# Attention and a cosine feed-forward on one core: plain float32 products for nine pairs of heads, and scalings moved between engines

## The chip, the cores and the metric

The kernel runs on one core of a Trainium2 chip. The metric is the device time of one execution in microseconds (us). Five engines work side by side, each through its own queue in order: PE (matrix products; PEld are its weight loads), DVE (vector), ACT (scalar, with the exponent), POOL (GpSimd), and SP, which here only issues transfers. Products are written to PSUM, the other tiles lie in SBUF.

## The reference

Eight batches, twelve heads, 448 positions, head size 64. q and k are divided by the root mean square of their rows and multiplied by g_q and g_k, then comes attention, then a feed-forward layer whose activation is h cos(h):

```python
rms = np.sqrt(np.mean(x * x, axis=-1, keepdims=True) + 1e-06)   # q_n, k_n = x / rms * g
scores = scale * np.matmul(q_n, k_n.transpose(0, 1, 3, 2))
attn = np.exp(scores - np.max(scores, axis=-1, keepdims=True))
attn = attn / (np.sum(attn, axis=-1, keepdims=True) + 1e-09)
x = np.matmul(attn, v)              # to [3584, 768]
h = x @ w_in                        # [3584, 2048]
y = (h * np.cos(h)) @ w_out         # [3584, 768]
```

## The kernel before

The 96 heads are worked on as 48 pairs, two heads side by side in the 128 partitions; six pairs make one batch b. The program has two parts. The first holds attention of all pairs and the first feed-forward product (L571 to L573) of batches 0 to 6, whose blocks lie between the attention pieces of the next batch; the second (from about 940 us) holds the product of the last batch, the activation and the second product (L646 to L648).

**Precision.** A matrix product with float32 accuracy is made in one of two ways. Split: both operands are cut into a part rounded to float32r (hi) and the remainder (lo), and three products hi·hi, lo·hi, hi·lo are summed. Plain: one product of float32 tiles, with no remainders to prepare. `S32` lists the pairs whose scores are plain, `A32` those whose product P v is plain. Before, these are pairs 0 and 1, and 0 to 11.

**Preparation of a pair** (`prepare(u)`, from pair 2; pairs 0 and 1 take a path of their own, `first(u)`). ACT squares the rows of q and k, DVE sums them (L298), POOL adds the mean's 1e-6 (L302) and takes the power -1/2 (L306). SP stores these factors and loads them back spread over all partitions (`rkb` for k, `rqb` for q). Then POOL multiplies k by its factors (L370), ACT casts k to hi (L373), POOL makes its remainder `kl` (L377). For q POOL first multiplies by g_q g_k / 8 with a minus sign (`q_scale`, L385, in place), then by its factors (L389); ACT casts it to `qhi` (L392), POOL makes `ql` (L396). A pair in `S32` has no `kl`, `ql` and no casts: POOL writes `khi` and `qhi` itself. `kd`, `qd`, `rkb`, `rqb` have one buffer each, `khi`, `qhi`, `kl`, `ql` two.

**Attention of a pair** (`attend(u)`). Seven tiles of scores: column group j holds the tiles j and j + 4, tile 3 stands alone (L438); three PSUM banks and one shared with the feed-forward hold them. DVE takes the minimum of each row (L447; the scores carry a minus sign), ACT the exponent with the row sum (L456). `rsum` adds 1e-9 to the row sums (L463) and inverts them (L464), both on DVE. Then four blocks kc of 128 keys: PE transposes P into `PT` (L481), which has one buffer of two halves; for a plain pair ACT copies the first half to SBUF (L492) and DVE the second (L490), and PE multiplies by v (L520). For a split pair ACT casts both halves, DVE makes the remainders `lo` (L500, L502), and PE multiplies both (L512); v is cut by POOL (L409, L413), and the two heads' outputs are joined by ACT and DVE (L538, L543) and scaled on POOL (L546). A plain pair is scaled by one row on DVE (L530). POOL then makes the remainder of the output `xs` (L557), the input of the feed-forward.

**Weights.** The weights come as 64-bit numbers. DVE decodes each of 16 blocks of w_in in four steps (L216, L218, L220, L224), ACT casts (L234), POOL makes the remainder (L239, two halves). The decoded block `wf` has two buffers: step L216 of a block waits for L239 of the block two before. w_out follows later (L224 with 384 columns among others).

**What sets the order.** Every piece is added to a planner with its engine, an estimated cost, a due time and the keys that it reads and writes. The planner runs through the pieces, gives each engine the ready piece that is due first, and writes the program in that order; the hardware queues then keep it. A changed cost or engine thus moves pieces far from the change as well.

Of the kernel before, what the change touches and what calls it, by code (L numbers as in the profile page):

```python
# [10 lines left out]
F32 = mybir.dt.float32  # L11
F32R = mybir.dt.float32r
I32 = mybir.dt.int32
AF = mybir.ActivationFunctionType
ALU = mybir.AluOpType
# [111 lines left out]
def tile_attention_moe(  # L127
# [11 lines left out]
    nc = tc.nc  # L139
# [7 lines left out]
    S32, A32 = (0, 1), tuple(range(12))  # L147
# [234 lines left out]
    def q_scale(u):  # L382
        qd = pair[u]["qd"]
        q = tl(u, "qhi", [128, 512], F32) if u in S32 else qd
        nc.gpsimd.tensor_scalar(q, qd, gsc, 0.0, op0=ALU.mult, op1=ALU.add)  # L385
# [5 lines left out]
    def q_high(u):  # L391
        nc.scalar.copy(tl(u, "qhi", [128, 512], F32R), pair[u]["qd"])  # L392

    def q_low(u):
        d = pair[u]
        nc.gpsimd.tensor_tensor(tl(u, "ql", [128, 512], F32R), d.pop("qd"), d["qhi"].bitcast(F32), ALU.subtract)  # L396
# [64 lines left out]
    def rsum(u):  # L461
        sm = pair[u]["sm"]
        nc.vector.tensor_scalar(sm[:, 3, :], sm[:, 2, :], 1.0, 1e-9, op0=ALU.mult, op1=ALU.add)  # L463
        nc.vector.reciprocal(sm[:, 3, :], sm[:, 3, :])  # L464
# [20 lines left out]
    def pt_high(u, kc, hh):  # L485
        d = pair[u]
        dt = F32 if u in A32 else F32R
        hi = d["hi", kc, hh] = apool.tile([128, S], dt, tag="hi", name=f"hi{u}_{kc}_{hh}", bufs=RING["hi"])
        if u in A32 and hh == 1:
            nc.vector.tensor_copy(hi, pt[:, hh * S : hh * S + S])  # L490
        else:
            nc.scalar.copy(hi, pt[:, hh * S : hh * S + S])  # L492
# [259 lines left out]
    def prepare(u):  # L752
# [18 lines left out]
        if u in S32:  # L771
            add(POOL, 0.8, D0 - 16, q_scale, u, r=[("gsc", 0)] + qd, w=qhi)
        else:
            add(POOL, 0.8, D0 - 20, q_scale, u, r=[("gsc", 0)], w=qd)
            add(POOL, 1.33, D0 - 16, q_norm, u, r=[("rqb", u)], w=qd)
            add(ACT, 0.6, D0 - 10, q_high, u, r=qd, w=qhi)
            add(POOL, 1.33, D0 - 8, q_low, u, r=qd + qhi, w=[("ql", u)])
# [9 lines left out]
    def attend(u):  # L787
# [4 lines left out]
        for j in range(4):  # L792
# [3 lines left out]
            cost = (1.55 if j < 3 else 0.8) if u in S32 else (0.88 if j < 3 else 0.62)  # L796
# [12 lines left out]
        add(DVE, 0.6, D1 + 3, rsum, u, r=[("sm", u, 2, t) for t in range(7)], w=[("sm", u, 3)])  # L809
        for kc in range(4):  # L810
# [14 lines left out]
            for hh in range(2):  # L825
                n = 8 * u + 2 * kc + hh
                eng, cost = (DVE, 0.62) if u in A32 and hh else (ACT, 0.53)
# [235 lines left out]
```

## Time and profile before

| | |
|---|---|
| median of three executions | 1458.5 us (1457.64, 1458.5, 7169.15) |
| profiled execution, own time | 1460.09 us |
| its span | 1458.2 us |
| mean granted clock of PE | 0.99 |
| instructions | 22619 |

Busy time in the profiled span: PE 1409.4 us (97%), DVE 1006.8 (69%), ACT 978.6 (67%), POOL 1015.3 (70%). A row of a timeline reads: start, time, engine, line, operation, output <- input, partitions x elements, count, and in brackets the idle time of the engine before it with what ended it. A row of the groups by line gives the busy time in all and the mean of one, then the idle time before. Products on PE overlap, so the durations of single rows sum to more than the time that passes; for PE the distance from start to start is what counts. A plain float32 product stands as two rows. The granted clock is a share of PE's full clock.

### The profile page before, as it was taken

The numbers are of one execution on the slowest core, as the hardware profiler recorded it, in microseconds if no ns is written. First come the engines' busy times: TensorE is split into PE (matmuls) and PEld (weight loads), VectorE is DVE, ScalarE is ACT, GpSimd is POOL, SyncE is SP. The second block draws the span as 40 slices with busy tenths as digits, with TensorE's granted clock in tenths as the row PEclk, the third lists the DMA queues.
The fourth block names the chain that finished last, engine by engine and source line by source line (L and its number), as shares of the span: only waits on it lengthen the run. The fifth ranks groups of instructions, "written<-read, shape, count | busy, mean of one in ns | idle before, by whom it ended". The sixth has DMA issues, their size and how long they took to land.

```text
span 1458.2 us, 22619 instructions
## 1 busy us (share of the span) xinstructions
PE 1409.4 (97%) x7416; PEld 1158.0 (79%) x7416; DVE 1006.8 (69%) x1652; ACT 978.6 (67%) x1990; POOL 1015.3 (70%) x806
## 2 busy tenths in 40 slices
PE   7888999999999999999999999999999999999999
PEld 3444667888878888878888788889989889899898
DVE  6788985568687776767586755436876876976821
ACT  4666665767777777676667676537786786776742
POOL 5879887767999898886777584111285596585684
PEclk9899999999999999999999999999999999999999
DMA  6677555455667576736555443129669569479373
GB/s 199 190 216 251 166 148 152 141 165 181 203 202 231 181 220 197 224 126 202 179 177 179 150 164 93 59 88 349 226 206 317 201 220 340 151 250 338 128 243 100
DMA packets 154021, 282.63 MB, mean 194 GB/s; under 512 B 31712, under 2 KB 101552, under 8 KB 153904
## 3 DMA queue, kind: packets, MB, share of 16 engines
q1 hardware_dynamic: 153904, 281.20, 59.8%
q8 instruction: 58, 0.95, 0.3%
q14 instruction: 59, 0.48, 0.1%
HBM read 218.24 MB, written 62.89 MB: 193 GB/s over the span
## 4 chain that ended last, share of the span: by engine, by line
PE 72%; DVE 12%; POOL 5%; ACT 4%; issue 4%; DMA 3%; SPq 0%; ACTq 0%; POOLq 0%; DVEq 0%
PE ph L571 9%; PE PT L481 9%; PE ph L572 8%; PE ph L573 8%; PE S L438 7%; PE O L512 7%; PE y L647 7%; PE y L648 7%; PE y L646 7%; PE O L520 2%; DMA hb<-h_d 1%; POOL glo L631 1%; ACT hi L492 1%; DVE sm L447 1%; DVE lo L500 1%
## 5 line engine op out<-in xcount | busy, mean ns | idle before, releaser
L571 PE MATMUL ph<-xs,wi 128*128 128x448 f32 x768 | 299.5, 390 | 2.3 <-ACT he L583 2.3
L572 PE MATMUL ph<-xs,wi 128*128 128x448 f32 x768 | 282.0, 367 | 0.2 <-POOL xs L557 0.2
L573 PE MATMUL ph<-xs,wi 128*128 128x448 f32 x768 | 281.7, 367 | 0.0
L456 ACT ACTIVATE P<-S,sm 128x448 f32<-128x448 f32 x336 | 213.2, 639 | 94.2 <-DVE sm L447 84.3
L647 PE MATMUL y<-glo,wo 128*128 128x448 f32 x672 | 247.1, 368 | 6.2 <-POOL glo L631 6.2
L646 PE MATMUL y<-ghi,wo 128*128 128x448 f32 x672 | 246.6, 367 | 0.0
L648 PE MATMUL y<-ghi,wo 128*128 128x448 f32 x672 | 246.6, 367 | 0.0
L492 ACT CAST hi<-PT 128x448 fp32r<-128x448 f32 x288 | 141.6, 536 | 99.1 <-PE PT L481 54.4
L447 DVE TENSOR_REDUCE sm<-S 128x1 f32<-128x448 f32 x322 | 187.2, 612 | 26.8 <-PE S L438 26.1
L481 PEld LDWEIGHTS PT<-ident,P 128*128 128x128 f32 x1344 | 156.4, 142 | 51.1 <-issue 34.5
L481 PE MATMUL PT<-ident,P 128*128 128x128 f32 x1344 | 185.3, 279 | 3.2 <-DVE hi L490 3.2
L500 DVE TENSOR_TENSOR lo<-PT,hi 128x448 fp32r<-128x448 f32 x216 | 124.6, 617 | 78.8 <-ACT hi L492 78.3
L571 PEld LDWEIGHTS ph<-xs,wi 128*128 128x128 f32 x768 | 144.9, 189 | 33.2 <-issue 13.0
L573 PEld LDWEIGHTS ph<-xs,wi 128*128 128x128 f32 x768 | 144.7, 188 | 12.8
L572 PEld LDWEIGHTS ph<-xs,wi 128*128 128x128 f32 x768 | 145.3, 189 | 10.2 <-POOL xs L557 0.6
L647 PEld LDWEIGHTS y<-glo,wo 128*128 128x128 f32 x672 | 126.6, 188 | 18.5 <-POOL glo L631 7.7
L306 POOL TENSOR_TENSOR r<-r,nhalf 128x14 f32<-128x14 f32 (+1 forms) x50 | 129.6, 2594 | 12.4 <-DVE r L324 8.7
L646 PEld LDWEIGHTS y<-ghi,wo 128*128 128x128 f32 x672 | 126.6, 188 | 11.0
L648 PEld LDWEIGHTS y<-ghi,wo 128*128 128x128 f32 x672 | 126.6, 188 | 10.9
L438 PE MATMUL S<-khi,qhi 64*128 64x448 f32 (+1 forms) x350 | 103.3, 498 | 9.4 <-ACT P L456 6.6
L512 PE MATMUL O<-hi,vs 128*128 128x448 f32 x288 | 93.1, 379 | 2.1 <-DVE xf L543 1.2
L512 PE MATMUL O<-lo,vs 128*128 128x448 f32 x216 | 82.8, 399 | 6.4 <-DVE lo L500 6.1
(225 smaller groups left out, 2826.3 us busy)
## 6 DMA issues: line engine op xcount, KB each, us to landing
wo<-wo_d SPq DMA_DIRECT2D x88, 768.0 KB
h_d<-he SPq DMA_DIRECT2D x128, 224.0 KB
hb<-h_d SPq DMA_DIRECT2D x64, 448.0 KB
wo_d<-wv SPq DMA_DIRECT2D x56, 384.0 KB
sd<-sd SPq DMA_DIRECT2D x46, 448.0 KB
qd<-qT SPq DMA_DIRECT2D x48, 256.0 KB
raw<-w_in SPq DMA_DIRECT2D x16, 768.0 KB
rawo<-w_out SPq DMA_DIRECT2D x32, 384.0 KB
```

The costliest lines, as they stand in the source:

```text
L438: nc.tensor.matmul(d["S", t][:, :S], d[a][p0:p1, j * 128 : j * 128 + 128], d[c][p0:p1, :], start=(n == 0), stop=(n == len(ops) - 1),)
L447: nc.vector.tensor_reduce(least, d["S", t][:, :S], axis=AX.X, op=ALU.min)
L456: nc.scalar.activation(tl(u, f"P{t}", [128, S], F32, "P"), d.pop(("S", t))[:, :S], AF.Exp, bias=sm[:, 1, t : t + 1], scale=-1.0, accum_out ...
L481: nc.tensor.transpose(pt[:, t * 128 : t * 128 + 128], src, ident)
L492: nc.scalar.copy(hi, pt[:, hh * S : hh * S + S])
L512: nc.tensor.matmul(O, st, d.pop((what, kb, hh)), start=(kc + n == 0), stop=(kc + n == 4))
L571: nc.tensor.matmul(ph[:, :S], whi, x2[:, 0, :], start=(cc == 0), stop=False)
L572: nc.tensor.matmul(ph[:, :S], whi, x2[:, 1, :], start=False, stop=False)
L573: nc.tensor.matmul(ph[:, :S], wlo, x2[:, 0, :], start=False, stop=(cc == NCC - 1))
L646: nc.tensor.matmul(y, whi, hi, start=(k == 0 and chain < 2), stop=False, skip_group_check=chain == 2)
L647: nc.tensor.matmul(y, whi, lo, start=False, stop=False, skip_group_check=chain == 2)
L648: nc.tensor.matmul(y, wlo, hi, start=False, stop=(k == NH - 1), skip_group_check=chain == 2)
```

## The change

- `S32` and `A32` become pairs 0 to 8. Scores of pairs 2 to 8 become plain; P v of pairs 9 to 11 becomes split.
- The multiplication of q by g_q g_k leaves POOL for pairs from 2 on: ACT applies it in the cast to `qhi`, and the remainder `ql` is made by one DVE instruction, q times factor minus `qhi`, instead of a POOL subtraction.
- `rsum` is cut in two: ACT adds the 1e-9, DVE inverts.
- Of the eight copies of P of a plain pair, the one of the second half in the last block of keys goes from DVE to ACT: five on ACT, three on DVE.
- The planner's costs follow.

```diff
-    S32, A32 = (0, 1), tuple(range(12))
+    S32, A32 = tuple(range(9)), tuple(range(9))
...
     def q_scale(u):
-        qd = pair[u]["qd"]
-        q = tl(u, "qhi", [128, 512], F32) if u in S32 else qd
-        nc.gpsimd.tensor_scalar(q, qd, gsc, 0.0, op0=ALU.mult, op1=ALU.add)
+        nc.gpsimd.tensor_scalar(tl(u, "qhi", [128, 512], F32), pair[u].pop("qd"), gsc, 0.0, op0=ALU.mult, op1=ALU.add)
...
     def q_high(u):
-        nc.scalar.copy(tl(u, "qhi", [128, 512], F32R), pair[u]["qd"])
+        nc.scalar.activation(tl(u, "qhi", [128, 512], F32 if u in S32 else F32R), pair[u]["qd"], AF.Copy, scale=gsc)
 
     def q_low(u):
         d = pair[u]
-        nc.gpsimd.tensor_tensor(tl(u, "ql", [128, 512], F32R), d.pop("qd"), d["qhi"].bitcast(F32), ALU.subtract)
+        nc.vector.scalar_tensor_tensor(
+            tl(u, "ql", [128, 512], F32R), d.pop("qd"), gsc, d["qhi"].bitcast(F32), op0=ALU.mult, op1=ALU.subtract
+        )
...
-    def rsum(u):
+    def rsum(u, step):
         sm = pair[u]["sm"]
-        nc.vector.tensor_scalar(sm[:, 3, :], sm[:, 2, :], 1.0, 1e-9, op0=ALU.mult, op1=ALU.add)
-        nc.vector.reciprocal(sm[:, 3, :], sm[:, 3, :])
+        if step == 0:
+            nc.scalar.activation(sm[:, 3, :], sm[:, 2, :], AF.Copy, bias=1e-9, scale=1.0)
+        else:
+            nc.vector.reciprocal(sm[:, 3, :], sm[:, 3, :])
...
-        if u in A32 and hh == 1:
+        if u in A32 and hh == 1 and kc < 3:
             nc.vector.tensor_copy(hi, pt[:, hh * S : hh * S + S])
...
-        if u in S32:
-            add(POOL, 0.8, D0 - 16, q_scale, u, r=[("gsc", 0)] + qd, w=qhi)
-        else:
-            add(POOL, 0.8, D0 - 20, q_scale, u, r=[("gsc", 0)], w=qd)
-            add(POOL, 1.33, D0 - 16, q_norm, u, r=[("rqb", u)], w=qd)
-            add(ACT, 0.6, D0 - 10, q_high, u, r=qd, w=qhi)
-            add(POOL, 1.33, D0 - 8, q_low, u, r=qd + qhi, w=[("ql", u)])
+        add(POOL, 1.33, D0 - 16, q_norm, u, r=[("rqb", u)], w=qd)
+        add(ACT, 0.72, D0 - 10, q_high, u, r=[("gsc", 0)] + qd, w=qhi)
+        if u not in S32:
+            add(DVE, 0.75, D0 - 8, q_low, u, r=[("gsc", 0)] + qd + qhi, w=[("ql", u)])
...
-            cost = (1.55 if j < 3 else 0.8) if u in S32 else (0.88 if j < 3 else 0.62)
+            cost = (1.05 if j < 3 else 0.86) if u in S32 else (0.88 if j < 3 else 0.62)
...
-        add(DVE, 0.6, D1 + 3, rsum, u, r=[("sm", u, 2, t) for t in range(7)], w=[("sm", u, 3)])
+        add(ACT, 0.22, D1 + 2, rsum, u, 0, r=[("sm", u, 2, t) for t in range(7)], w=[("sm", u, 3)])
+        add(DVE, 0.21, D1 + 3, rsum, u, 1, w=[("sm", u, 3)])
...
-                eng, cost = (DVE, 0.62) if u in A32 and hh else (ACT, 0.53)
+                eng, cost = (DVE, 0.62) if u in A32 and hh and kc < 3 else (ACT, 0.53)
```

## Prediction

> **What bounds the kernel now.** I read the busy time of the engines by stage first, since one average over 1458 us mixes three stages, then the timeline of PE with the idle time before each row, and for each long gap the rows of DVE and POOL just ahead of it. By stage (columns: window, its length, then busy us of PE, PEld, DVE, ACT, POOL, each with its instructions, granted clock, DMA share):
>
> ```profile
> 0.00:20.00 20.00, 10.00 (x25) 4.96 (x26) 10.02 (x25) 8.41 (x15) 10.55 (x14) 1.00 0.71 246
> 20.00:200.00 180.00, 161.88 (x780) 92.54 (x779) 154.86 (x231) 114.51 (x256) 147.03 (x112) 0.93 0.63 195
> 200.00:940.00 740.00, 731.45 (x4143) 599.12 (x4141) 503.14 (x891) 516.92 (x1201) 568.08 (x549) 1.00 0.55 172
> 940.00:1458.00 518.00, 506.10 (x2475) 461.41 (x2471) 338.81 (x507) 338.71 (x521) 289.62 (x132) 1.00 0.66 223
> ```
>
> From 200 us on PE works almost without a gap (731.45 of 740, then 506.10 of 518). There only PE's own work counts; DVE (68%) and POOL (77%) have room. From 20 to 200 us no engine is full: PE 161.88 of 180 at a clock of 0.93, DVE 154.86, POOL 147.03. So that stage has 18.1 us of idle PE, and its clock gives away up to 0.07 of 161.88, 11.3 us. About 29 us is thus all that relief of POOL and DVE can bring there; the first 20 us hold the loads and the two special pairs, which the change hardly touches.
>
> The longest gap in that stage shows who causes it. In order: PE, then DVE, then POOL.
>
> ```profile
> 127.56 0.74 PE L438 MATMUL S<-khi,qhi 64*128 64x448 f32 x1 [4.55 <-ACT P L456]
> 127.56 1.11 PE L438 MATMUL S<-khi,ql 64*128 64x448 f32 x2
> ...
> 123.36 1.49 DVE L216 TENSOR_SCALAR wf<-raw 128x768 int32<-128x768 int32 x1 [2.68 <-POOL wi L239]
> 124.76 1.26 DVE L463 TENSOR_SCALAR sm<-sm 128x7 f32<-128x7 f32 x1
> 126.18 1.10 DVE L447 TENSOR_REDUCE sm<-S 128x1 f32<-128x448 f32 x2
> ...
> 104.82 0.69 POOL L385 TENSOR_SCALAR qd<-qd,gs 128x512 f32<-128x512 f32 x1 [1.10 <-DMA qd<-qT]
> 108.91 1.17 POOL L377 TENSOR_TENSOR kl<-kd,khi 128x448 fp32r<-128x448 f32 x1
> 110.03 1.30 POOL L396 TENSOR_TENSOR ql<-qd,qhi 128x512 fp32r<-128x512 f32 x1
> 118.65 0.69 POOL L385 TENSOR_SCALAR qd<-qd,gs 128x512 f32<-128x512 f32 x1
> 122.33 0.99 POOL L239 TENSOR_TENSOR wi<-wf,wi 128x384 fp32r<-128x384 f32 x1
> ```
>
> PE waited 4.55 us for a score bank. Named is ACT's exponent, but that had waited for DVE's row minimum (126.18), which stood behind the weight decode at L216; that waited 2.68 us until POOL's remainder of older weights (L239, end 123.3) gave the buffer free. POOL was late because the preparation rows of q and k shown here stand ahead of L239 in its queue. The seven-column DVE row L463 took 1.26 us here, against a mean of 0.478 us below.
>
> **The change part by part.** Per-instruction prices, from the groups by line (busy us, mean ns | idle before, releaser):
>
> ```profile
> L385 POOL TENSOR_SCALAR qd<-qd,gs 128x512 f32<-128x512 f32 x46 | 38.0, 826 | 1.8 <-DMA qd<-qT 1.4 <-DMA vd<-v 0.3
> L396 POOL TENSOR_TENSOR ql<-qd,qhi 128x512 fp32r<-128x512 f32 x46 | 62.7, 1364 | 4.9 <-ACT qhi L392 4.9
> L377 POOL TENSOR_TENSOR kl<-kd,khi 128x448 fp32r<-128x448 f32 x46 | 54.6, 1187 | 41.0 <-ACT khi L373 37.7 <-DMA rs<-rs_d 3.1
> L463 DVE TENSOR_SCALAR sm<-sm 128x7 f32<-128x7 f32 x48 | 23.0, 478 | 5.3 <-ACT P L456 4.2
> L490 DVE COPY hi<-PT 128x448 f32<-128x448 f32 x48 | 29.5, 614 | 16.9 <-ACT hi L492 16.7
> L492 ACT COPY hi<-PT 128x448 f32<-128x448 f32 x48 | 25.5, 531 | 38.9 <-PE PT L481 26.1 <-PE PT L483 10.9 <-issue 1.3
> L224 DVE SCALAR_TENSOR_TENSOR wx<-rawo,wx 128x384 f32<-128x384 f32 x32 | 23.0, 724 | 1.2 <-ACT rawo L222 1.2
> L512 PEld LDWEIGHTS O<-lo,vs 128*128 128x128 f32 x216 | 40.5, 187 | 26.9 <-DVE lo L500 23.9
> ```
>
> POOL: a pair of 2 to 8 loses the scaling of q, the remainder of q and that of k, 0.83 + 1.36 + 1.19 = 3.38 us, 23.7 us for seven pairs in the stage where POOL shows 147 us. Here is POOL's order around the preparation of pair 7 (r: root mean squares; xs: split of a finished output; wi: remainder of a weight block), before:
>
> ```order
> L302 TENSOR_SCALAR r8_970<-r8_970 128x14
> L306 TENSOR_TENSOR r8_970<-r8_970,nhalf_94 128x14
> L370 TENSOR_TENSOR kd7_945<-kd7_945,rkb7_918 128x448
> L385 TENSOR_SCALAR qd7_958<-qd7_958,gs_93 128x512
> L389 TENSOR_TENSOR qd7_958<-qd7_958,rqb7_931 128x512
> L557 TENSOR_TENSOR xs_502<-xf3_949,xs_502 128x448
> L239 TENSOR_TENSOR wi4_982<-wf4_727,wi4_982 128x384
> L377 TENSOR_TENSOR kl7_1061<-kd7_945,khi7_1046 128x448
> L396 TENSOR_TENSOR ql7_1079<-qd7_958,qhi7_1050 128x512
> L239 TENSOR_TENSOR wi4_982<-wf4_727,wi4_982 128x384
> ```
>
> and now:
>
> ```order
> L302 TENSOR_SCALAR r8_885<-r8_885 128x14
> L306 TENSOR_TENSOR r8_885<-r8_885,nhalf_94 128x14
> L370 TENSOR_TENSOR khi7_918<-kd7_795,rkb7_831 128x448
> L387 TENSOR_TENSOR qd7_869<-qd7_869,rqb7_847 128x512
> L559 TENSOR_TENSOR xs_464<-xf3_861,xs_464 128x448
> L239 TENSOR_TENSOR wi3_905<-wf3_641,wi3_905 128x384 x2
> L559 TENSOR_TENSOR xs_464<-xf4_995,xs_464 128x448
> L239 TENSOR_TENSOR wi4_1023<-wf4_738,wi4_1023 128x384
> ```
>
> Three rows of ten are gone. New is that L370 writes khi itself, a buffer of two, so POOL now waits there until PE has finished the scores of pair 5; the next q, xs and wi stand behind it.
>
> Gap at 123 to 127: the four removed POOL rows ahead of L239 sum to 0.69 + 1.17 + 1.30 + 0.69 = 3.85 us, and L463's 1.26 us moves to ACT: 5.1 us, more than the gap. I take all 4.5 us, and 1.5 us for the slow products behind it (L438 rows of 1.11 us there, 0.37 us below). The second gap, in the order PE, DVE, POOL:
>
> ```profile
> 81.40 1.54 PE L481 MATMUL PT<-ident,P 128*128 128x128 f32 x7 [3.15 <-DVE hi L490]
> ...
> 72.04 0.95 DVE L218 SCALAR_TENSOR_TENSOR wf<-raw,wf 128x768 int32<-128x768 int32 x1
> 77.04 1.79 DVE L218 SCALAR_TENSOR_TENSOR wf<-raw,wf 128x768 int32<-128x768 int32 x1
> 78.87 1.94 DVE L220 SCALAR_TENSOR_TENSOR wf<-raw,wf 128x768 int32<-128x768 int32 x1
> ...
> 75.44 1.15 POOL L377 TENSOR_TENSOR kl<-kd,khi 128x448 fp32r<-128x448 f32 x1
> 77.98 2.01 POOL L396 TENSOR_TENSOR ql<-qd,qhi 128x512 fp32r<-128x512 f32 x1
> ```
>
> L218 takes 0.95 us at 72.04 and 1.79 us at 77.04, where POOL's k remainder runs; L220 behind it, beside the q remainder, 1.94 us. Both POOL rows go. Of the 3.15 us I take 2.5. The other gaps of the stage (18.1 - 4.55 - 3.15 = 10.4 us): 2 us. Gain in sum: 4.5 + 1.5 + 2.5 + 2 = 10.5 us; its bounds are 0 and the 29 us above.
>
> PE: each plain score or P v product is two rows in the trace.
>
> ```profile
> 10.66 4.24 PE L438 MATMUL S<-khi,qhi 64*128 64x448 f32 x8 [1.18 <-ACT khi L343]
> 32.31 1.02 PE L438 MATMUL S<-khi,qhi 64*128 64x448 f32 x4
> 33.26 1.55 PE L520 MATMUL O<-hi,vs 128*64 128x448 f32 x4
> 69.72 0.47 PE L438 MATMUL S<-khi,qhi 64*128 64x448 f32 x2
> 70.03 0.37 PE L438 MATMUL S<-khi,ql 64*128 64x448 f32 x2
> 70.52 1.56 PE L520 MATMUL O<-hi,vs 128*64 128x448 f32 x4
> ...
> 240.52 0.91 PE PT L481 x7
> 243.28 0.90 PE O L520 x4
> 251.02 0.81 PE O L512 x4
> 251.84 0.77 PE PT L481 x7
> ```
>
> From start to start, two plain tiles take 33.26 - 32.31 = 0.95 us and two tiles of three split products 70.52 - 69.72 = 0.80 us. So plain scores are dearer for PE by 0.15 us, four times a pair, seven pairs: +4.2 us. At the rate of the start (4.24 us for eight rows) it would be 14 x 0.53 = 7.4 us a pair instead of 3.2, +29 us; the warm row is nearer to this place. Pairs 9 to 11 go the other way: P v from 4 x 0.90 = 3.6 us to 14 x 0.81 / 4 = 2.84 us, their transposes from 0.91 to 0.77 us four times: -1.3 us each, -4.0 us. PE's work stays within +0.2 us.
>
> ACT takes the fourth P copy of nine pairs, 0.53 us, from DVE's 0.61 us: both copies of that block now follow each other on one engine, so P v can start up to 0.53 us later, 4.8 us at most, 0 at least; I take a third, +1.5. The 1e-9 becomes a seven-column row on ACT, whose other work (114.51 of 180 us, then 516.92 of 740) hides it; uncovered it is at most L463's 0.478 us, 48 times, 23 us. The scale in ACT's cast of q adds no instruction. Pairs 9 to 11 get eight remainders of P each back on DVE and four rows of v on POOL, just ahead of the 251 us at which L512 shows up now, so where PE is the bound: nothing, else at most 24 x 0.61 = 15 us. SP issues three more loads of v.
>
> DVE gets the remainder of q of 39 pairs. The nearest row, L224, the same operation on two tiles of 384 columns, has 0.724 us; for 512 columns that makes 0.97 us. DVE loses L463's 0.478 us a pair, so its load grows by 0.49 us in some 19 us (740 us over 39 pairs). Its order where the pair before is transposed (sm: row minima and sums, lo: remainders of P), before:
>
> ```order
> L447 TENSOR_REDUCE sm19_4034<-S19_0_4035 128x1
> L543 TENSOR_TENSOR xf17_4045<-O17_3831,xf17_4045 64x448
> L500 TENSOR_TENSOR lo18_0_0_4085<-PT_98,hi18_0_0_4072 128x448
> L500 TENSOR_TENSOR lo18_0_1_4088<-PT_98,hi18_0_1_4075 128x448
> L447 TENSOR_REDUCE sm19_4034<-S19_4_4036 128x1
> L467 COPY rt18_4135<-PT_98 7x128
> L500 TENSOR_TENSOR lo18_1_0_4139<-PT_98,hi18_1_0_4124 128x448
> ```
>
> and now:
>
> ```order
> L447 TENSOR_REDUCE sm19_3935<-S19_4_3937 128x1
> L502 TENSOR_TENSOR lo18_0_0_3990<-PT_98,hi18_0_0_3986 128x448
> L502 TENSOR_TENSOR lo18_0_1_4002<-PT_98,hi18_0_1_3988 128x448
> L394 SCALAR_TENSOR_TENSOR ql20_4015<-qd20_3765,gs_93,qhi20_4004 128x512
> L469 COPY rt18_4041<-PT_98 7x128
> L502 TENSOR_TENSOR lo18_1_0_4045<-PT_98,hi18_1_0_4028 128x448
> ```
>
> The new row stands ahead of a remainder that PE's P v waits for. PE waits for such rows 23.9 us over 216 now (L512 above). Bounds: 0, and every 0.97 us on PE's path, 39 x 0.97 = 38 us; 0.11 us a remainder speaks for the low end: +2.
>
> Sum: -10.5 + 0.2 + 1.5 + 2 = -6.8 us. The profiled execution took 1460.09 us with a span of 1458.2; its span is 0.3 us below the median, 1458.5, to which I apply the sum: **1451.7 us**.
>
> A rule speaks against the move to DVE. The Trainium skill (SBUF — State Buffer, section Who interferes with whom) says that a VectorE instruction with two SBUF inputs and a GpSimd instruction that reads SBUF exclude each other for a whole instruction. The decodes above agree; the power row does not:
>
> ```profile
> 128.65 2.58 POOL L306 TENSOR_TENSOR r<-r,nhalf 128x14 f32<-128x14 f32 x1
> 129.25 0.94 DVE L218 SCALAR_TENSOR_TENSOR wf<-raw,wf 128x768 int32<-128x768 int32 x1
> ```
>
> By the rule the decode inside POOL's 2.58 us would have been held; it took its plain 0.94 us. By the rule the remainder of q behind a power row would cost up to 2.6 us more, and (2) below would be likelier; by the row it isn't.
>
> **The rivals.** (1) *POOL's relief is hidden.* In the stage before 200 us each pair's chain of transpose, copy and P v on PE sets the pace, POOL now waits for PE at L370, and the time POOL saves becomes idle. For it: the gap is ended by ACT and DVE, DVE is the busier of the two; against: L216's 2.68 us wait names POOL. Then 3 us of the two long gaps go and 3.7 us are added: 1459.
>
> (2) *Slower: the remainder of q holds up PE's P v from 200 us on.* DVE goes in order; place: between the remainders of P, as shown. It decides once more than about 9 us of its 38 reach PE, for the rest gains 8.8. At half: 1449.7 + 19 = 1469. Against it: DVE at 68% has room and PE has other products queued between.
>
> (3) *The stage before 200 us closes up.* All 18.1 us of gaps and the clock's 11.3 go: 1458.5 - 29.4 + 3.7 = 1433. For it: gaps and slow clock share one cause here; against: pairs still follow one another through one transpose buffer.
>
> **How the numbers follow.** The forecast has 0.50, (1) 0.23, (2) 0.13, (3) 0.14. The forecast's own range is 1443 to 1460: half the gain more, or none. The range reaches towards (3) and (2): 1434 to 1470. A change of 2%, 29 us, is about what a measurement of this kernel can tell from none. Faster by that (under 1429.3) needs more than (3): 0.05. Slower (over 1487.7) needs all 38 us of (2): 0.03. Within: 0.92.
>
> **What would show it.** Right: between 20 and 200 us POOL's busy time per pair falls by about 3.4 us, no gap of PE over 3 us, a clock above 0.93; plain scores from start to start near 0.95 us; PE's wait for remainders of P near 24 us. Wrong: PE idle of 18 us or more in that stage with POOL idle beside it (1); PE's wait for lo above 45 us and a busy share of PE below 98% from 200 to 940 (2); the gap gone and PE full from 100 us on (3). Plain scores at 1.5 us a pair of tiles would break the sum on its PE side.

## The result, and the profile after

The changed kernel takes 1450.6 us (median of six, 1448.93 to 1452.87). The kernel before took 1455.40 to 1463.12 us in five of the six runs beside it; the sixth, 7169 us, is left out. The ratio is 0.9941, 95% interval 0.9918 to 0.9964, so 8.6 us less. The forecast was 1451.7 us and less than 2% of change, and both came. The sum was right, but two of its terms were not: the early stage gained twice what I gave it, and a part of that was lost in pairs 9 to 11 and in the steady stage.

The profiled execution, the lowest of the six, took 1448.93 us with a span of 1447.1. By stage (columns as before: busy us of PE, PEld, DVE, ACT, POOL, then granted clock and DMA share):

```profile
0.00:20.00 20.00, 9.82 (x25) 4.97 (x26) 9.93 (x25) 8.24 (x15) 10.38 (x14) 1.00 0.73 246
20.00:200.00 180.00, 167.36 (x825) 96.77 (x824) 152.52 (x233) 131.69 (x296) 128.57 (x98) 0.99 0.67 202
200.00:940.00 740.00, 726.04 (x4107) 600.11 (x4106) 524.62 (x899) 529.72 (x1246) 506.00 (x481) 1.00 0.55 171
940.00:1447.00 507.00, 493.77 (x2409) 450.86 (x2407) 333.70 (x494) 331.98 (x503) 287.66 (x131) 1.00 0.68 227
```

Between 20 and 200 us POOL has 18 us less, PE's idle time falls from 18.1 to 12.6 us and its clock rises from 0.93 to 0.99. From 200 to 940 us PE's idle time grows, from 8.6 to 14.0 us. Stages cut at fixed times do not hold the same work in the two kernels, though. A better yardstick is the copy of a pair's row sums on DVE (L467, now L469), which comes once a pair. At pair 6, before any block of the feed-forward is finished, it stands at 132.92 us before and at 112.25 now: 20.7 us earlier. At pair 14, where in every kernel below 20 blocks are done, the lead is 17.1 us; at pair 47, the last, 12.9; at the end of the span 11.1. The stretch up to pair 6, first before, then now:

```profile
0.00:132.92 132.92, 106.46 (x462) 53.81 (x464) 102.91 (x174) 81.73 (x183) 99.11 (x83) 0.92 0.69 214
```
```profile
0.00:112.22 112.22, 94.29 (x421) 43.51 (x421) 85.08 (x154) 79.23 (x182) 69.36 (x58) 1.00 0.77 234
```

PE's idle time there falls from 26.5 to 17.9 us and its busy time by 12.2 us, while its clock goes from 0.92 to 1.00; a clock of 0.92 over 132.92 us is a loss of some 10 us. POOL has 30 us less to do. The places of the two long gaps, the transposes of pair 3 and the scores of pair 7, look like this now:

```profile
67.45 1.02 PE L438 MATMUL S<-khi,qhi 64*128 64x448 f32 x4
68.89 0.98 PE L483 MATMUL PT<-ident,P 128*128 128x128 f32 x7 [0.42 <-DVE hi L492]
...
107.60 1.02 PE L438 MATMUL S<-khi,qhi 64*128 64x448 f32 x2
108.84 1.02 PE L438 MATMUL S<-khi,qhi 64*128 64x448 f32 x2 [0.23 <-ACT P L456]
```

The gaps of 3.15 and 4.55 us have become 0.42 and 0.23. But a new one stands where pair 9, now the first with split P v, begins. In the order PE, DVE, ACT, POOL:

```profile
169.56 0.37 PE L575 MATMUL ph<-xs,wi 128*128 128x448 f32 x1
172.58 0.44 PE L514 MATMUL O<-hi,vs 128*128 128x448 f32 x1 [2.65 <-ACT hi L494]
176.03 1.70 PE L483 MATMUL PT<-ident,P 128*128 128x128 f32 x7
...
167.39 1.78 DVE L218 SCALAR_TENSOR_TENSOR wf<-raw,wf 128x768 int32<-128x768 int32 x1
169.21 1.92 DVE L220 SCALAR_TENSOR_TENSOR wf<-raw,wf 128x768 int32<-128x768 int32 x1
...
171.16 0.91 ACT L222 ACTIVATE raw<-raw 128x768 f32<-128x768 f32 x1 [4.00 <-DVE wf L220]
171.97 0.94 ACT L494 CAST hi<-PT 128x448 fp32r<-128x448 f32 x2
...
168.32 2.00 POOL L387 TENSOR_TENSOR qd<-qd,rqb 128x512 f32<-128x512 f32 x1
170.28 1.17 POOL L409 TENSOR_SCALAR vs<-vd 128x320 fp32r<-128x320 f32 x1
```

Read it upwards: PE waits for the cast of P (L494); the cast stands on ACT behind the square of a weight block (L222), which waited 4.00 us for DVE's decode; the decode took 1.78 and 1.92 us beside POOL's rows, where it takes 0.94 alone. Behind the gap PE runs at half its clock (transposes of 1.70 us against 0.98). Last the groups by line that the forecast named, PE's weight load for a remainder of P, DVE's remainder of q and POOL's k:

```profile
L514 PEld LDWEIGHTS O<-lo,vs 128*128 128x128 f32 x234 | 44.0, 188 | 32.6 <-DVE lo L502 28.9
L514 PE MATMUL O<-lo,vs 128*128 128x448 f32 x234 | 89.3, 397 | 10.3 <-DVE lo L502 9.8
L394 DVE SCALAR_TENSOR_TENSOR ql<-qd,gs,qhi 128x512 fp32r<-128x512 f32 x39 | 37.9, 972 | 4.5 <-ACT qhi L390 4.0
L370 POOL TENSOR_TENSOR khi<-kd,rkb 128x448 f32<-128x448 f32 x7 | 10.4, 1489 | 0.3 <-DMA rkb<-r_d 0.3
```

PE's wait for remainders of P is 28.9 us (23.9 before), the remainder of q has a mean of 0.972 us, and POOL waits 0.3 us at L370, not for PE.

### The profile page after: what moved, and what is told of

Its sections match the earlier page's. It is cut to its first block, busy times and chain, and to the rows that moved or that the text cites. A ratio compares the mean times of both kernels' runs of the same rounds, so it can differ in the third digit from the quotient of the medians.

```text
span 1447.1 us, 22426 instructions
## 1 busy us (share of the span) xinstructions
PE 1397.0 (97%) x7361; PEld 1152.7 (80%) x7361; DVE 1020.8 (71%) x1649; ACT 1001.6 (69%) x2058; POOL 932.6 (64%) x722
## 4 chain that ended last, share of the span: by engine, by line
PE 71%; DVE 14%; ACT 5%; DMA 4%; issue 4%; POOL 2%; SPq 0%; ACTq 0%; DVEq 0%; POOLq 0%
PE ph L573 9%; PE PT L483 8%; PE ph L574 8%; PE ph L575 8%; PE O L514 8%; PE S L438 7%; PE y L649 7%; PE y L650 7%; PE y L648 7%; DVE lo L502 2%; DMA hb<-h_d 2%; ACT hi L494 1%; POOL glo L633 1%; DVE sm L447 1%; PE O L522 1%
## 5 line engine op out<-in xcount | busy, mean ns | idle before, releaser
L494 ACT CAST hi<-PT 128x448 fp32r<-128x448 f32 x312 | 153.5, 536 | 93.9 <-PE PT L483 49.6
L502 DVE TENSOR_TENSOR lo<-PT,hi 128x448 fp32r<-128x448 f32 x234 | 134.7, 617 | 71.5 <-ACT hi L494 70.2
L483 PE MATMUL PT<-ident,P 128*128 128x128 f32 x1344 | 181.2, 275 | 3.0 <-DVE hi L492 3.0
L575 PEld LDWEIGHTS ph<-xs,wi 128*128 128x128 f32 x768 | 144.2, 188 | 12.6
L649 PEld LDWEIGHTS y<-glo,wo 128*128 128x128 f32 x672 | 126.6, 188 | 19.4 <-POOL glo L633 8.7
L648 PEld LDWEIGHTS y<-ghi,wo 128*128 128x128 f32 x672 | 126.6, 188 | 11.7 <-ACT ghi L635 0.7
L438 PE MATMUL S<-khi,qhi 64*128 64x448 f32 x399 | 115.0, 518 | 1.7 <-ACT khi L343 1.2
L514 PE MATMUL O<-hi,vs 128*128 128x448 f32 x312 | 101.9, 381 | 7.3 <-ACT hi L494 3.3
L514 PE MATMUL O<-lo,vs 128*128 128x448 f32 x234 | 89.3, 397 | 10.3 <-DVE lo L502 9.8
```

The lines of the kernel that those rows point to most:

```text
L438: nc.tensor.matmul(d["S", t][:, :S], d[a][p0:p1, j * 128 : j * 128 + 128], d[c][p0:p1, :], start=(n == 0), stop=(n == len(ops) - 1),)
L483: nc.tensor.transpose(pt[:, t * 128 : t * 128 + 128], src, ident)
L514: nc.tensor.matmul(O, st, d.pop((what, kb, hh)), start=(kc + n == 0), stop=(kc + n == 4))
L575: nc.tensor.matmul(ph[:, :S], wlo, x2[:, 0, :], start=False, stop=(cc == NCC - 1))
L648: nc.tensor.matmul(y, whi, hi, start=(k == 0 and chain < 2), stop=False, skip_group_check=chain == 2)
L649: nc.tensor.matmul(y, whi, lo, start=False, stop=False, skip_group_check=chain == 2)
```

## The experiments

Theory A, from the prediction: POOL's preparation of q and k holds up the weights' decode and, through it, PE; its relief is the gain. The rivals are named with the runs by letters: the gain comes from the small moves off DVE (B), from the order of the rows that the planner happens to give (G); the granted clock is the loss (E) or the gap alone (F); the remainder of q costs PE something later (C) or nothing (D). All results in one table; the ratio is to the kernel before in the same runs (medians 1457.6 to 1457.9 us there). The leads are those of the row-sum copy over the kernel before, in one profiled execution each (a minus: earlier). An execution can lie off its median, by -8.9 us in e5_qlow_pool and by +6.0 in e2_qmove; the stretch from pair 14 to 47 is steadier, 0.3 us apart in the three executions that have the rows of the kernel before there (that kernel, e8_fill, e12_fill_short). The last column is span times one minus the clock, a mean over all timed runs, 13.4 to 13.7 us for the kernel before.

| run | median us | ratio (95%) | pair 6 | pair 14 | pair 47 | clock us |
|---|---|---|---|---|---|---|
| the changed kernel | 1450.6 | 0.9941 (0.9918 to 0.9964) | -20.7 | -17.1 | -12.9 | 6.8 |
| e1_scores | 1458.6 | 1.0003 (0.9985 to 1.0022) | -7.1 | -7.7 | -7.1 | 12.7 |
| e2_qmove | 1456.2 | 0.9987 (0.9968 to 1.0006) | -4.8 | -2.0 | -0.6 | 9.3 |
| e3_small | 1453.4 | 0.9983 (0.9965 to 1.0002) | -0.2 | -6.6 | -7.1 | 9.3 |
| e4_pv12 | 1448.2 | 0.9934 (0.9916 to 0.9951) | -21.0 | -20.4 | -12.7 | 4.6 |
| e5_qlow_pool | 1449.1 | 0.9936 (0.9912 to 0.9961) | -21.2 | -15.8 | -15.6 | 5.7 |
| e6_qlow_twice | 1461.5 | 1.0020 (1.0006 to 1.0034) | -21.0 | -13.2 | +0.7 | 8.5 |
| e7_costs | 1439.1 | 0.9873 (0.9853 to 0.9892) | -21.6 | -21.8 | -19.4 | 4.6 |
| e8_fill | 1471.5 | 1.0084 (1.0063 to 1.0105) | +5.3 | +6.4 | +6.7 | 10.0 |
| e9_before_costs | 1456.0 | 0.9983 (0.9967 to 0.9998) | -6.9 | -3.0 | -3.2 | 7.1 |
| e10_pool_back | 1468.1 | 1.0081 (1.0051 to 1.0111) | +0.5 | +4.4 | +7.2 | 17.4 |
| e11_costs_pv12 | 1434.0 | 0.9838 (0.9814 to 0.9862) | -20.9 | -21.7 | -27.3 | 4.0 |
| e12_fill_short | 1458.7 | 1.0010 (0.9990 to 1.0030) | +0.7 | -0.9 | -0.6 | 13.4 |

### One part of the change alone

The planner's costs follow in each of these runs; the diffs show the operations, and `...` marks what is left out.

**Plain scores for pairs 2 to 8, nothing else (e1_scores).**

```diff
-    S32, A32 = (0, 1), tuple(range(12))
+    S32, A32 = tuple(range(9)), tuple(range(12))
...
     def q_norm(u):
...
-        nc.gpsimd.tensor_tensor(qd, qd, pair[u].pop("rqb"), ALU.mult)
+        q = tl(u, "qhi", [128, 512], F32) if u in S32 else qd
+        nc.gpsimd.tensor_tensor(q, qd, pair[u].pop("rqb"), ALU.mult)
```

> The kernel before with one part of the change alone: pairs 2 to 8 get plain float32 scores, so POOL loses the remainders of k and q of seven pairs (2.55 us a pair) and no other edit is made (POOL still scales q, P v is plain for the first twelve pairs as before, nothing is added to DVE). Theory A (POOL's preparation of q and k delays the decode of the weights on DVE, and through it the row minima and PE): most of the lead that the changed kernel has at pair 8 (20.5 us at its row-sum copy) shows here too, 12 to 20 us, and since nothing loads DVE later, most of it lasts to pair 47: 1445 to 1451 us. Theory B (the lead comes from the small moves off DVE, the 1e-9 and the fourth copy, not from POOL): lead at pair 8 below 5 us, 1456 to 1462 us.

Neither came whole: the lead, 7.1 us at pair 6 and 7.3 at pair 8, lies between the two, and the time is that of the kernel before, as theory B had it. Pairs 4 to 8 (from the row-sum copy of pair 3 to that of pair 8), here, then in the changed kernel:

```profile
75.33:167.44 92.11, 85.35 (x383) 45.85 (x382) 85.82 (x116) 59.47 (x123) 78.98 (x59) 0.96 0.75 227
```
```profile
70.59:154.28 83.69, 79.56 (x391) 44.14 (x389) 69.16 (x101) 62.41 (x138) 62.88 (x46) 1.00 0.83 251
```

DVE (third busy column) is busy 85.82 of 92.11 us here, 69.16 of 83.69 in the changed kernel. In this order 14 of the 16 weight blocks are begun on DVE by pair 8, in the changed one 11, in the kernel before 12. POOL gave room, and DVE, at 93% as full as PE, is likely the next bound; no run tests that alone.

**The scaling and the remainder of q alone (e2_qmove).**

```diff
-        nc.scalar.copy(tl(u, "qhi", [128, 512], F32R), pair[u]["qd"])
+        nc.scalar.activation(tl(u, "qhi", [128, 512], F32R), pair[u]["qd"], AF.Copy, scale=gsc)
...
-        nc.gpsimd.tensor_tensor(tl(u, "ql", [128, 512], F32R), d.pop("qd"), d["qhi"].bitcast(F32), ALU.subtract)
+        nc.vector.scalar_tensor_tensor(
+            tl(u, "ql", [128, 512], F32R), d.pop("qd"), gsc, d["qhi"].bitcast(F32), op0=ALU.mult, op1=ALU.subtract
+        )
```

> The kernel before with only the scaling of q moved into ACT's cast and its remainder to DVE, for pairs 2 to 47 (the scores stay split from pair 2 on, so pairs 2 to 8 too have a remainder of q on DVE). POOL loses 2.19 us a pair, DVE gains 0.97 us a pair. Theory A: a part of the lead at pair 8, 4 to 10 us, since POOL is relieved but DVE, the busier engine there, is loaded; from 200 us on the lead shrinks by 3 to 6 us as remainders of P stand behind the new row: 1454 to 1460 us. Theory B: no lead at pair 8 (below 3 us) and a loss later: 1460 to 1466 us.

As theory A had it: 6.1 us at pair 8, gone by pair 47, 1456.2 us, a ratio that cannot be told from one.

**The 1e-9 and the fourth copy alone (e3_small).**

```diff
-        nc.vector.tensor_scalar(sm[:, 3, :], sm[:, 2, :], 1.0, 1e-9, op0=ALU.mult, op1=ALU.add)
...
+            nc.scalar.activation(sm[:, 3, :], sm[:, 2, :], AF.Copy, bias=1e-9, scale=1.0)
...
-        if u in A32 and hh == 1:
+        if u in A32 and hh == 1 and kc < 3:
```

> The kernel before with only the small moves: the 1e-9 as a row on ACT for all pairs, the fourth P copy of the pairs with plain P v (the first twelve here) on ACT. POOL is as before. Theory A: lead at pair 8 below 4 us, 1457 to 1462 us. Theory B: DVE's relief (1.26 us of a seven-column row ahead of the long gap, 0.61 us a copy) makes the lead: 8 us or more at pair 8, 1446 to 1453 us.

Between the two: no lead at pair 6 and 5.8 us at pair 8; the ratio, 0.9983, is 2.5 us with an interval that reaches one, and the medians lie 4.3 us apart. Theory B is out as the main cause, but these moves are no loss either; I had put +1.5 us on them.

The three parts sum to 4 us by their ratios, the whole change to 8.6. At pair 6 they sum to 12 us, the whole to 20.7. This suggests that relief of POOL and of DVE pay together more than each alone; but each of these runs has an order of its own, so the sum is not clean.

### POOL's load given back, in the order of the changed kernel

```diff
         nc.gpsimd.tensor_tensor(k, kd, pair[u].pop("rkb"), ALU.mult)
+        if 2 <= u < 9:
+            nc.gpsimd.tensor_tensor(kd, kd, kd, ALU.subtract)
...
         nc.gpsimd.tensor_tensor(qd, qd, pair[u].pop("rqb"), ALU.mult)
+        if 2 <= u < 9:
+            for _ in range(2):
+                nc.gpsimd.tensor_tensor(pair[u]["kd"], pair[u]["kd"], pair[u]["kd"], ALU.subtract)
```

> The changed kernel, with the order of all its rows kept, and POOL's relief taken back: for pairs 2 to 8 POOL gets three more rows of 128x448 each (a difference of k's tile with itself, used by nobody; one behind the normalised k, two behind the normalised q), some 3.5 us a pair where the change took away 3.4. Theory A (POOL's load between 33 and 155 us holds up the decode, and through it PE): the lead at pair 8 falls from 20.5 us to 10 or less, and the time rises to 1455 to 1462 us. Theory G (the gain comes from the order of the rows that the planner's run happens to give, not from POOL's load): the lead stays above 16 us, and the time within 1449 to 1453 us.

In this run, e10_pool_back, the lead at pair 6 is gone, +0.5 us for -20.7, and the time is 1468.1 us, 17.5 above the changed kernel and more than theory A had expected. The order is the same row for row, and where it differs ahead of pair 6 with the whole change in place (e7_costs, e11_costs_pv12) the lead there stays 21.6 and 20.9 us: theory G is out for the early stage. The largest gap, in the order PE, DVE, POOL:

```profile
109.51 0.74 PE L579 MATMUL ph<-xs,wi 128*128 128x448 f32 x1 [6.04 <-POOL xs L564]
...
111.41 0.56 DVE L216 TENSOR_SCALAR wf<-raw 128x768 int32<-128x768 int32 x1 [2.49 <-POOL wi L239]
...
103.11 1.13 POOL L370 TENSOR_TENSOR khi<-kd,rkb 128x448 f32<-128x448 f32 x1 [4.65 <-DMA rkb<-r_d]
104.32 0.93 POOL L372 TENSOR_TENSOR kd<-kd 128x448 f32<-128x448 f32 x1
105.21 1.26 POOL L389 TENSOR_TENSOR qd<-qd,rqb 128x512 f32<-128x512 f32 x1
106.42 1.94 POOL L392 TENSOR_TENSOR kd<-kd 128x448 f32<-128x448 f32 x2
108.33 1.13 POOL L564 TENSOR_TENSOR xs<-xf,xs 128x448 fp32r<-128x448 f32 x1
109.42 1.95 POOL L239 TENSOR_TENSOR wi<-wf,wi 128x384 fp32r<-128x384 f32 x2
```

Three unused rows (L372 and twice L392) put 2.9 us ahead of POOL's xs, for which PE waits 6.04 us, and of wi, for which DVE's decode waits 2.49 us. The normalised k at the head had itself waited 4.65 us for the load of `rkb`, and the added rows cause this too. They read and write `kd`, which has one buffer, so SP can issue the next load of k only when they end, and the load of `rkb` stands behind it in SP's queue:

```profile
90.86 1.94 POOL L392 TENSOR_TENSOR kd<-kd 128x448 f32<-128x448 f32 x2
...
92.82 0.33 SPq L365 DMA_DIRECT2D kd<-kT  x1
94.20 1.09 SPq L353 DMA_DIRECT2D rkb<-r_d  x2
```

(SPq is SP's queue.) SP waited 5.2 us at L365 for L392 here. Between 50 and 170 us such waits sum to 20.5 us; at the same load the changed kernel waits 4.9 us for L370 (50 to 155 us), the kernel before 3.5 for L377 (50 to 165 us). So this run gives back more than the change took: POOL's time, and a hold on the loads that is four times as long as in either kernel. It shows that rows in POOL's queue can cost PE the whole lead; what their time alone costs was not tried.

### What was lost after pair 6

**Plain P v for pairs 9 to 11 again (e4_pv12).**

```diff
-    S32, A32 = tuple(range(9)), tuple(range(9))
+    S32, A32 = tuple(range(9)), tuple(range(12))
```

> The changed kernel with plain P v for the first twelve pairs again instead of nine. In the changed kernel the lead over the kernel before falls from 20.5 us at pair 8 to 13.8 at pair 11. Theory A1 (the three newly split pairs cause this: eight remainders of P each on DVE, four rows of v on POOL, and PE waiting for them): the fall goes away, lead at pair 12 of 17 to 21 us, 1445 to 1449 us. Theory A2 (the lead is lost there anyway, because PE is the bound from there on and has the same work left to do; plain P v costs PE 1.3 us a pair more): lead at pair 12 of 9 to 14 us, 1450 to 1455 us.

A1: the lead at pair 12 is 18.9 us where the changed kernel has 13.2, the gap ahead of pair 9 and the half clock behind it are gone, and the median is 2.4 us lower. The stretch from pair 8 to pair 12, first here, then in the changed kernel:

```profile
153.40:234.43 81.03, 79.76 (x438) 55.56 (x437) 58.50 (x87) 53.07 (x119) 55.74 (x47) 1.00 0.45 137
```
```profile
154.28:240.16 85.88, 81.33 (x452) 65.02 (x450) 68.00 (x103) 60.05 (x133) 64.50 (x57) 0.98 0.42 129
```

PE has 1.3 us of idle time instead of 4.5. The 5.7 us won there do not all last: up to pair 29 the lead stays 2.6 us ahead, and from pair 32 on the two are level (14.1 and 14.2 us), in an order of rows that differs there too. So the split pairs cost 4.9 us from pair 8 to pair 12 in this order; in that of e7_costs and e11_costs_pv12 below, which differ in the same pairs, the stretch takes 85.0 and 83.1 us, 1.9 less. The 2.4 us of the medians are a sum with the order.

**The remainder of q on POOL (e5_qlow_pool), and twice on DVE (e6_qlow_twice), both in the order of the changed kernel.**

```diff
-        nc.vector.scalar_tensor_tensor(
-            tl(u, "ql", [128, 512], F32R), d.pop("qd"), gsc, d["qhi"].bitcast(F32), op0=ALU.mult, op1=ALU.subtract
-        )
+        qd = d.pop("qd")
+        nc.gpsimd.tensor_scalar(qd, qd, gsc, 0.0, op0=ALU.mult, op1=ALU.add)
+        nc.gpsimd.tensor_tensor(tl(u, "ql", [128, 512], F32R), qd, d["qhi"].bitcast(F32), ALU.subtract)
```

> The changed kernel, in its own order, with the remainder of q of pairs 9 to 47 issued on POOL instead of DVE, as a scaling and a difference (some 2.2 us a pair on POOL, 0.97 us less on DVE). Pairs 2 to 8 are as in the changed kernel. Theory C (DVE's remainder of q delays the remainders of P that PE waits for, and this gives back 3 to 5 us after 200 us): PE's wait for remainders of P falls from 38.7 us in all (28.9 for DVE, 9.8 behind PE) to about 30, and the time to 1445 to 1449 us. Theory D (DVE has room, the remainder costs nothing): 1449 to 1453 us, and with POOL's load back it may be up to 3 us slower than the changed kernel.

```diff
...
+        ql, qd = tl(u, "ql", [128, 512], F32R), d.pop("qd")
+        for _ in range(2):
+            nc.vector.scalar_tensor_tensor(ql, qd, gsc, d["qhi"].bitcast(F32), op0=ALU.mult, op1=ALU.subtract)
```

> The changed kernel, in its own order, with the remainder of q of pairs 9 to 47 computed twice on DVE, one row behind the other (39 rows of 0.97 us more, 37.9 us). Theory C: PE's wait for remainders of P grows to 45 us or more, and the time by 3 to 12 us: 1454 to 1463 us. Theory D: the second row too is hidden, 1449 to 1453 us.

PE's weight load of a remainder of P, on POOL first, then twice on DVE:

```profile
L514 PEld LDWEIGHTS O<-lo,vs 128*128 128x128 f32 x234 | 43.9, 188 | 27.6 <-DVE lo L502 24.3
```
```profile
L514 PEld LDWEIGHTS O<-lo,vs 128*128 128x128 f32 x234 | 44.1, 188 | 41.2 <-DVE lo L502 37.9
```

Without the row on DVE the wait is 24.3 us, with one 28.9, with two 37.9 (with the waits on PE itself 32.7, 38.7 and 53.1). Between pairs 14 and 47 the lead shrinks by 0.2, 4.2 and 13.9 us. So the row costs about 4 us, a second one 9.7: theory C, at a tenth of the row's 37.9 us for the first and a quarter for the second. In the medians the second row is plain (1461.5 us), the first is not: 1449.1 against 1450.6, in runs that spread from 1440 to 1457, and with POOL's load back.

### The planner's order

**The changed kernel, two estimated costs altered (e7_costs).**

```diff
-        add(ACT, 0.72, D0 - 10, q_high, u, r=[("gsc", 0)] + qd, w=qhi)
+        add(ACT, 0.66, D0 - 10, q_high, u, r=[("gsc", 0)] + qd, w=qhi)
...
-        add(ACT, 0.22, D1 + 2, rsum, u, 0, r=[("sm", u, 2, t) for t in range(7)], w=[("sm", u, 3)])
+        add(ACT, 0.25, D1 + 2, rsum, u, 0, r=[("sm", u, 2, t) for t in range(7)], w=[("sm", u, 3)])
```

> The changed kernel with two of the planner's costs altered and no operation changed (the cast of q from 0.72 to 0.66, the row of the 1e-9 from 0.22 to 0.25), so that only the order of the rows differs here and there. If the order that the planner happens to give is worth little: 1449 to 1453 us. If it is worth as much as the parts of the change: 2.5 us or more away from 1450.6, to either side.

It is 11.5 us faster than the changed kernel with the same operations: more than the change itself brought. Up to pair 6 the two are alike (21.6 and 20.7 us of lead). The difference opens between pairs 7 and 14, 4.7 us, and grows to 6.5 at pair 47 and 8.6 at the end of the spans, 3 us short of the medians'. Here 10 weight blocks are begun by pair 8 instead of 11, and no gap of PE over 1.03 us is left between 110 and 240 us. How much of it each of the two explains was not tried.

**The kernel before, two costs altered (e9_before_costs).**

```diff
-            add(ACT, 0.6, D0 - 10, q_high, u, r=qd, w=qhi)
+            add(ACT, 0.66, D0 - 10, q_high, u, r=qd, w=qhi)
...
-        add(DVE, 0.6, D1 + 3, rsum, u, r=[("sm", u, 2, t) for t in range(7)], w=[("sm", u, 3)])
+        add(DVE, 0.5, D1 + 3, rsum, u, r=[("sm", u, 2, t) for t in range(7)], w=[("sm", u, 3)])
```

> The kernel before with two of the planner's costs altered and no operation changed (the cast of q from 0.6 to 0.66, the row of the 1e-9 with the reciprocal from 0.6 to 0.5). In the changed kernel two such alterations were worth 11 us. Theory G (the order alone is worth about 10 us to either side, whichever kernel it is): a time 4 us or more away from 1457.7. Otherwise (the order matters only in the changed kernel): 1455 to 1460 us.

Worth 2.5 us by the ratio, with an interval up to 5, and 1456.0 us as expected without theory G: this one alteration moved the kernel before little. Two samples are few; what they allow to say is that a difference of 8.6 us between two such kernels may hold several us of order, and that only a run with the order held (e5_qlow_pool, e6_qlow_twice, e10_pool_back) is free of it.

**Both that were faster together (e11_costs_pv12).**

```diff
-    S32, A32 = tuple(range(9)), tuple(range(9))
+    S32, A32 = tuple(range(9)), tuple(range(12))
...
-        add(ACT, 0.72, D0 - 10, q_high, u, r=[("gsc", 0)] + qd, w=qhi)
+        add(ACT, 0.66, D0 - 10, q_high, u, r=[("gsc", 0)] + qd, w=qhi)
...
-        add(ACT, 0.22, D1 + 2, rsum, u, 0, r=[("sm", u, 2, t) for t in range(7)], w=[("sm", u, 3)])
+        add(ACT, 0.25, D1 + 2, rsum, u, 0, r=[("sm", u, 2, t) for t in range(7)], w=[("sm", u, 3)])
```

> The changed kernel with both alterations that were faster than it: plain P v for the first twelve pairs (1448.2) and the two other planner's costs (1439.1). If the split P v of pairs 9 to 11 costs what it did before (2.4 us) whatever the order: 1435 to 1438 us. If the order that results decides (theory G): anywhere from 1438 to 1455 us.

1434.0 us, the fastest of all, 1 us below the first range: 0.9838 of the kernel before. The waits for remainders of P, on PEld and on PE:

```profile
L514 PEld LDWEIGHTS O<-lo,vs 128*128 128x128 f32 x216 | 40.5, 187 | 22.6 <-DVE lo L502 19.1
L514 PE MATMUL O<-lo,vs 128*128 128x448 f32 x216 | 82.5, 393 | 4.6 <-DVE lo L502 4.4
```

They sum to 23.5 us; with plain P v alone they are 27.7 and 11.2, 38.9 us. This difference of 15.4 us is close to the 13.3 us by which the two kernels part between pairs 14 and 47, and to the 14.3 us of their medians. So between these two the order seems to decide how often DVE's other rows, the remainder of q among them, stand ahead of a remainder of P. It is no rule: with the altered costs alone the waits are 28.2 and 11.7 us, 39.9, no less than the 38.7 of the changed kernel, and the time is 11.5 us lower all the same.

### Is the clock a loss of its own?

**Products that nobody uses, in four of PE's gaps of the kernel before (e8_fill, then e12_fill_short).** The result of the changed kernel suggested it: in the table the mean clock loss falls by about 7 us, nearly the whole gain.

```diff
+    AGAIN, FILL = {(7, 1, 0, 1): 18}, {(1, 3, 0, 3): 18, (4, 2, 2, 6): 36, (7, 3, 1): 16}
...
+    def fill(out, n):
+        for _ in range(n):
+            nc.tensor.matmul(out, ident, ident[:, :64], start=True, stop=True)
...
+                for _ in range(AGAIN.get((u, j, n, t), 0)):
+                    nc.tensor.matmul(d["S", t][:, :S], d[a][p0:p1, j * 128 : j * 128 + 128], d[c][p0:p1, :], start=True, stop=True)
...
+                fill(d["S", t][:, S:], FILL.get((u, j, n, t), 0))
...
+            fill(d["O"][:, 1, :64], FILL.get((u, kc, hh), 0))
```

> The kernel before, and nothing of the change: in four places between 36 and 166 us where its profile shows PE waiting, PE gets products whose results are used by nobody (18 of 64 columns after the scores of pair 1, 36 after those of pair 4, 18 repeats of the first product of a score tile of pair 7, 16 of 64 columns ahead of a P v product of pair 7; some 1.4, 2.7, 3.7 and 1.2 us). They wait for nothing new, and the gaps stay where they are, but PE is busy in them. Theory E (most of the gain is the granted clock: the gaps of the kernel before are each followed by 4 to 10 us at half clock, and over all runs so far the span times one minus the granted clock is 13.7 us in the mean for the kernel before, 6.8 for the changed one, 4.6 with plain P v for twelve pairs): that figure falls to 9 us or less and the time by 3 to 7 us, 1451 to 1455 us. Theory F (the gaps themselves are the loss, and the clock adds little): nothing is gained, 1457 to 1463 us.

A miss of mine: each product of 64 columns stands as two rows of 0.115 us, so that the fillings took 4.13, 8.25, 3.91 and 3.79 us and delayed what lay behind them (+5.3 us at pair 6). It tells neither theory from the other.

```diff
-    AGAIN, FILL = {(7, 1, 0, 1): 18}, {(1, 3, 0, 3): 18, (4, 2, 2, 6): 36, (7, 3, 1): 16}
+    AGAIN, FILL = {(7, 1, 0, 1): 16}, {(1, 3, 0, 3): 6, (4, 2, 2, 6): 12, (7, 3, 1): 5}
```

> The kernel before, with products that nobody uses in the same four gaps of PE as in the first such run, but now no longer than the gaps: there the products of 64 columns took 0.115 us a row and not 0.075 in pairs of rows, so that 8.25 us stood in a gap of 3.15. Now 6, 12, 16 repeats, and 5: some 1.4, 2.8, 3.3 and 1.2 us. Theory E (the half clock behind the gaps is most of the loss): span times one minus the clock falls from 13.7 to 9 us or less, the time to 1451 to 1455 us. Theory F: 1457 to 1463 us.

Now the fillings fit, and nothing is gained: 1458.7 us, a clock loss of 13.4 us as before. The two longest gaps of before, in PE's rows:

```profile
76.06 1.53 PE L489 MATMUL PT<-ident,P 128*128 128x128 f32 x7
77.52 0.74 PE L445 MATMUL S<-khi,qhi 64*128 64x448 f32 x2
79.94 2.89 PE L428 MATMUL S<-ident 128*128 128x64 f32 x24
...
123.23 3.56 PE L444 MATMUL S<-khi,qhi 64*128 64x448 f32 x16
128.28 0.74 PE L445 MATMUL S<-khi,qhi 64*128 64x448 f32 x1 [1.29 <-ACT P L464]
129.70 1.12 PE L489 MATMUL PT<-ident,P 128*128 128x128 f32 x4
```

The clock halves here too (products of 0.74 us where the full clock gives 0.47), once ahead of the filled gap, once behind it, with no idle time of PE over 1.3 us near. So theory E did not hold in the form that I gave it: filling the gaps brought neither the clock nor the time. What a full clock would be worth this run cannot tell, since the clock stayed low. Others bear on it: with the altered costs of the kernel before the mean clock loss falls to 7.1 us, that of the changed kernel, and the time by 2.5 us only; and e5_qlow_pool and e7_costs run at half clock from 18 to 25 us and still reach pair 6 at 111.69 and 111.30 us, the changed kernel, at full clock, at 112.25. So the clock loss is not a price to be added in full to that of the waits; what sets the clock stays open.

## Why the prediction was right, point by point

- **The early stage, -10.5 us: mis-sized, and one of its two paths was wrong.** By pair 6 the lead was 20.7 us, and both gaps that I took are gone. For the gap at 123 us the path stands: POOL's rows ahead of xs and wi, with the loads that they hold, can cost PE the lead again. For the gap at 78 us it does not. I had put 2.5 us on a faster decode there. The remainder of k ended at 76.59; it had slowed L216 (1.35 us at 75.65, 0.55 now), but the slow L218 at 77.04 stood beside xs (76.56), which stays, and then beside the remainder of q. And ahead of the same transposes L218 and L220 are as slow now, beside POOL's q and xs:

```profile
64.45 1.84 DVE L218 SCALAR_TENSOR_TENSOR wf<-raw,wf 128x768 int32<-128x768 int32 x1
66.33 1.91 DVE L220 SCALAR_TENSOR_TENSOR wf<-raw,wf 128x768 int32<-128x768 int32 x1
68.27 0.57 DVE L492 COPY hi<-PT 128x448 f32<-128x448 f32 x1
```

  The decode stands earlier: L218 starts 2.1 us ahead of the transposes before the gap (66.53), where it had started 1.2 us behind them (75.83). My reason gives 0.8 us of the 2.5, by L216; that the gap closed all the same was luck. In the stretch to pair 6 the idle time fell by 8.5 us, close to the 9 us of my gap terms, and PE's busy time by 12.2, for which I had 1.5 us of slow products: that term was too small. Some 10 us of clock loss go with it, but how much the clock itself is worth is not settled. The kernel before with altered costs (e9_before_costs), at a clock of 0.99 up to pair 6, is 6.9 us earlier there than the kernel before at the same idle time (26.8 us for 26.5).
- **Plain scores, +4.2 us: their price was right.** From start to start two tiles take 70.87 - 69.92 = 0.95 us, as forecast, and nothing of the rate of the start came:

```profile
69.92 1.02 PE L438 MATMUL S<-khi,qhi 64*128 64x448 f32 x4
70.87 1.72 PE L522 MATMUL O<-hi,vs 128*64 128x448 f32 x8
```

- **P v of pairs 9 to 11, -4.0 us and "nothing" for the eight remainders and the v rows: wrong in sign.** Plain again, they are 4.9 us shorter from pair 8 to pair 12, and the kernel is 2.4 us faster; in the other order the two figures are 1.9 and 5.1. I had placed the pairs where PE is the bound, by the first split row at 251 us. They stand at 154 to 240 us now, at the end of the stage in which DVE decodes and POOL prepares. The slow decode ahead of the new gap stands beside POOL's rows of k, q and v; what the v rows alone cost there was not tried.
- **The remainder of q, +2 us: about 4,** by the lead between pairs 14 and 47 with and without it, at a duration of 0.972 us for the 0.97 worked out from L224. Rival (2) names the place rightly; its price stays below the 9 us from which it decides. The signs that I gave for it were half met: PE's wait is 28.9 us and not 45, PE is busy 98.1% from 200 to 940 us.
- **The fourth copy, +1.5 us, and the 1e-9, 0: no loss shown.** Together they are -2.5 us by the ratio, from -5.1 to +0.3, in the order of the kernel with these edits alone.
- **Rival (1), POOL waiting for PE at L370: not seen,** 0.3 us, and that for a load.
- **Rival (3), the stage closes up: its size came, for a while.** 20.7 of its 29.4 us were there at pair 6; 3.6 us went by pair 14, 4.2 by pair 47 and 1.8 in the last stage, which differs by 6 us between executions of the same rows (499.5 in e5_qlow_pool, 505.6 in the changed kernel).
- **The rule on shared access to SBUF.** Three remainders of q ran inside a power row of 2.58 to 2.88 us and took 0.74 us each, where the shortest of all 39 is 0.70; the longest, 1.63, ran beside POOL rows on full tiles. This is the row's answer, not the rule's, for the power row, and the rule's for the others (the Trainium skill, SBUF — State Buffer, section Who interferes with whom). The mean of 0.972 already holds the second kind.

That the total was met to 1.1 us is luck: an underrated gain and an overlooked loss cancel. The range was sound; the sum was not as good as it looks.

## What to carry to other kernels

In a stage where no engine is full, look for the in-order queue whose rows stand ahead of the one that others wait for, and count them: the whole change, with 3.4 us a pair taken from POOL, gave PE 20.7 us by pair 6. Relief of one engine alone may pay little where the next one is as close to full (7.1 us at pair 6 and none at the end for plain scores alone, with DVE at 93%). Where a planner sets the order, a change also draws a new order, and that may be worth as much as the change (11.5 us here): hold the order to learn what an edit costs, and try several orders to find the time that the kernel can have. When load is given back to price it, see which buffers the added rows hold: here they also stopped the loads for 20.5 us, and the price, 17.5 us in the medians, came out at twice the gain of the change.

## What the runs showed of the hardware

PE's granted clock goes to 0.50 for 3 to 14 us at a time (3.41, 6.83, 10.24 or 13.65 us in these profiles, apart from one at the end of each span), behind gaps as short as 1.1 to 1.5 us (e1_scores), and not each time: a gap of 1.56 us at 135 us in e4_pv12 was followed by no such stretch. The Trainium skill (TensorE: Matmul & The Clock Gate, Part 1) names half the clock as the state behind an idle window of about 3.4 us. The half agrees with the trace; idle times of that length do not stand ahead of most of these stretches, and products put into the gaps did not prevent them. Decode rows of DVE (L218, L220) take up to 1.8 to 1.9 us beside POOL rows on full tiles and 0.94 to 0.96 alone. DVE rows inside a power row of POOL (2.58 to 3.46 us) keep their time: 0.91 to 0.96 us for the decode, 0.74 for the remainder of q.
